# Attention's output product: two fp32 halves on column places against one whole product of split terms on the full array, in every second stretch

## The chip, the core and the metric

The kernel runs on one core of a Trainium2 chip. The metric is the device time of one execution in microseconds (us), median of several runs. The engines named below are TensorE (PE, with its weight loads shown apart as PEld), VectorE (DVE), ScalarE (ACT), GpSimd (POOL) and SyncE (SP), which issues most DMAs. The profiled execution is one run of its own, with its own time.

## The reference: what is computed

```python
x = A_x                                              # 1 x 2048 x 448
g = sigmoid((x * gate_w).sum(-1, keepdims=True))
# a: attention, 16 query heads of 28, one key head and one value head
q = (x @ wq) as 16 heads;  k = x @ wk;  v = x @ wv
p = softmax(q k^T * 28 ** -0.5);  o = p v
a = concat(o) @ wo                                   # 448 -> 448
# b: token shift and MLP mixer
h  = gelu(layernorm(B_x) @ w1), shifted by +1, -1, +2, -2 tokens in four parts
x1 = B_x + shifted(h) @ w2
b  = x1 + gelu(layernorm(x1) @ w3) @ w4              # 448 -> 1792 -> 448
out = g * a + (1 - g) * b
```

All arrays are fp32. Products of fp32 data are made in two ways in this kernel. A plain fp32 matmul appears in the trace as two instructions, each of which streams its columns at half the pace (256 columns in 0.22 us, where 512 columns of a split term take 0.23). A product of split terms uses the type fp32r: each operand is cut into a high part (its value rounded to fp32r) and a low part (what is left), and three matmuls add up high x high, high x low and low x high, each at full pace.

## The kernel before, in words

There are three parts, one behind the other in time: the projections and the token mixing, the MLP, and, from 394 us on, attention. Within `manual_schedule` each engine executes its instructions in the order in which the program issues them, so the order of calls in the last loop is the order on each engine. SP's DMA queue is in order as well.

**Attention** has 16 units (`NU`). Unit `u` is one block of 512 tokens and one group of 4 heads (for the last four units `place` swaps the meaning of tile and group). Each unit has 8 stretches (`NV`), and stretch `k = 8 u + v` takes two tiles of 128 keys. A stretch of the loop at L1050 issues, in order:

- `exps` (L1011): `scores` of the first key tile into the banks `even` (three tiles of PSUM: `even[0]`, `even[1]` with two banks, `even[2]`), one bank for each head. The four heads lie on four row places of the array, with 28 to 30 rows each, 512 columns, in three rounds of split terms. Then ACT makes exponentials from `even[0]` and from `even[1]` (L1009), DVE copies `even[2]` to `pd` (L1015). Then the same for the second key tile in the banks `odd`: DVE copies `odd[1]` (L1018) and ACT makes exponentials of the three banks of `odd[0]`.
- `late_exps` (L1021): ACT's exponential of what DVE has copied.
- one job in a PSUM bank that has just been freed: in the first stretches a rest of the MLP (`w4_job`, `w4_half`), later the output product `wo`.
- `values` (L1034) of the stretch before: sums of p times v, in fp32, on four column places (head j gives rows 32 j to 32 j + 31), for two halves of 256 tokens and two key tiles. One key tile in one half is one call of `value`: four matmuls, which the trace shows as eight. DVE adds each half to `o` (L1032) as soon as it is there.
- on some stretches the work on the unit before: row sums to a DRAM tile and back as reciprocals (`sums_begin` at v = 0, `recip` at v = 1), and at v = 3 `norm`, in which DVE writes the normalised `on` (128 rows of head and value dimension x 512 tokens).

**The output product** of a unit is 512 tokens x 448 columns, with the 128 rows of its 4 heads as the contraction: four tiles `t` of 128 tokens. `wo_part` (L877) makes a part of it in fp32 with `on` as the stationary operand, on four column places of 32 tokens each. `wo_half` makes 224 of the 448 columns, one half in each stretch from k = 12 on: those of unit u - 1 for v = 4 to 7, and of unit u - 2 for v = 0 to 3. In the last unit, at v = 4, 5 and 6, whole tiles of unit 14 are made (`wo_job` with 448 columns). `wo_end` has DVE read the bank, scale it by the gate and add it to `ot` (`by_one`, L874); with the last group, SP stores `ot`.

**PSUM.** After the scores, `free` lists `even[0], even[2], even[1][:, 0], odd[1]`. The job takes the first of it, and `values` takes the first and the last of what is left. So with a job the product goes to `even[0]`, and the two halves of `values` go to `even[2]` and `odd[1]`; without one they go to `even[0]` and `odd[1]`.

**Other queues.** POOL splits the queries of unit u + 2 (`q_begin` at v = 6), which frees the buffer for the DMA of the next queries (`q_fetch`, on SP). There are three sets of probability tiles (`SETS`), taken in turn, one for each stretch. The tail behind the loop makes the last stretch, one last whole tile of unit 14 and the output product of unit 15.

Of the kernel before, what the change touches and what calls it, by code (L numbers as in the profile page):

```python
# [10 lines left out]
F32R = mybir.dt.float32r  # L11
AF = mybir.ActivationFunctionType
ALU = mybir.AluOpType
# [3 lines left out]
P = 128  # L17
S = 2048
D = 448
# [17 lines left out]
def f32(ap):  # L37
    return ap.bitcast(F32)
# [3 lines left out]
def gated_mix_kernel(  # L42
# [12 lines left out]
    nc = tc.nc  # L55
# [120 lines left out]
    def place(u, t):  # L176
        b, g = divmod(u, NG)
        return (4 * b + t, g) if b < NB - 1 else (4 * b + g, t)
# [25 lines left out]
    NU = NB * NG  # L204
# [56 lines left out]
    with tc.tile_pool(name="s1b", bufs=1) as s1b, \  # L261
# [35 lines left out]
        hh, hl, acts = {}, {}, {}  # L297
# [382 lines left out]
    with tc.tile_pool(name="s2", bufs=1, reuse_waits="tile") as s2, \  # L680
            tc.tile_pool(name="ps2", bufs=1, space=PSUM, reuse_waits="tile") as ps2:
        def weigh_x1(n0, n1):
            for n in range(n0, n1):
                nc.gpsimd.tensor_scalar(x1[:, n, :], x1[:, n, :], gi[:, n:n + 1], None, op0=ALU.mult)
# [43 lines left out]
        for b in range(NB):  # L728
            acc = [ps2.tile([P, 512], F32, tag="acc", bufs=4, name=f"acc_{b}_{t}") for t in range(4)]
            gs = {}  # L730
            for f in range(NF):
# [35 lines left out]
                u = M_AT.get(b * NF + f)  # L767
# [33 lines left out]
    with tc.tile_pool(name="s3", bufs=1, reuse_waits="tile") as s3, \  # L801
            tc.tile_pool(name="ps3", bufs=1, space=PSUM, reuse_waits="tile") as ps3:
        wof = s3.tile([P, 4, D], F32, name="wof")
# [7 lines left out]
        banks = []  # L811

        def take():
            return banks.pop(0)
# [8 lines left out]
        def q_fetch(u):  # L823
            if u >= NU:
                return
            raw = s3.tile([P, 512], F32, tag="qr", bufs=1, name=f"qr_{u}")
            if u < NU - NG:
                q_load(u, raw, 2 if u in TWO_PARTS else 1)
            else:
                q_load_last(u, raw)  # L830

        def q_begin(u):
            q_split(u, s3.tile([P, 512], F32R, tag="qh", bufs=3, name=f"qh_{u}"),
                    s3.tile([P, 512], F32R, tag="ql", bufs=3, name=f"ql_{u}"), nc.gpsimd)

        q_fetch(1)

        on_of = {}

        good = s3.tile([P, 16], F32, name="good")  # L840
        nc.gpsimd.memset(good, 1.0)
# [4 lines left out]
        def sums_begin(u, o):  # L846
            rt = s3.tile([P, 16], F32, tag="rt", bufs=2, name=f"rt_{u}")
            nc.sync.dma_start(rt, o[0:128:32, :].rearrange("j (a b) -> j a b", b=16))
            return u, o, rt
# [12 lines left out]
        def norm(u, o, rb):  # L862
            on_of[u] = s3.tile([P, 512], F32, tag="on", bufs=2, name=f"on_{u}")
            nc.vector.tensor_mul(on_of[u], o, rb)
# [12 lines left out]
        def wo_part(u, t, cols, ps, start, stop):  # L877
            for j in range(4):
                tok = slice(t * P + 32 * j, t * P + 32 * j + 32)
                nc.tensor.matmul(ps[32 * j:32 * j + 32, cols], on_of[u][:, tok], wof[:, place(u, t)[1], cols],  # L880
                                 start=start, stop=stop, tile_position=(0, 32 * j))

        def wo_end(u, t, ps, evict=by_one, queue=nc.sync, cols=slice(0, D)):
            n, g = place(u, t)
            before = x1[:, n, cols] if g == 0 else ot_of[n][:, cols]
            evict(n, ps, before, cols)
            store = out[0, n * P:(n + 1) * P, :], ot_of[n]
            if g == NG - 1 and cols.stop == D and queue:
                queue.dma_start(*store)
            return store  # L890

        def wo_job(u, t, cols=slice(0, D), evict=by_one, queue=nc.sync, ps=None):
            n, g = place(u, t)
            own = ps is None
            if own:
                ps = take()
            wo_part(u, t, cols, ps, True, True)
            if g == 0 and cols.start == 0:
                ot_of[n] = s3.tile([P, D], F32, tag="ot", bufs=5, name=f"ot_{n}")
            store = wo_end(u, t, ps, evict, queue, cols)  # L900
            if own:
                banks.append(ps)
            return store

        def wo_half(u, i, ps):
            t, h = divmod(i, 2)
            wo_job(u, t, slice(224 * h, 224 * h + 224), ps=ps)

        def w4_job(t, ps):
            n = NT - 4 + t  # L910
            tok = slice(t * P, (t + 1) * P)
            gh, gl = last_g
            ps = ps[:, 0:D]
            nc.tensor.matmul(ps, gh[:, tok], w4h[-1][:, 1, :], start=True, stop=False)
            nc.tensor.matmul(ps, gh[:, tok], w4l[-1][:, 1, :], start=False, stop=False)
            nc.tensor.matmul(ps, gl[:, tok], w4h[-1][:, 1, :], start=False, stop=True)
            nc.vector.tensor_add(x1[:, n, :], x1[:, n, :], ps)

        def w4_half(k, i, ps):
            t, h = divmod(i, 2)  # L920
            n = NT - 4 + t
            cols = slice(224 * h, 224 * h + 224)
            for j in range(4):
                tok = slice(t * P + 32 * j, t * P + 32 * j + 32)
                nc.tensor.matmul(ps[32 * j:32 * j + 32, cols], gf_late[k][:, tok], w4f[:, k, cols],
                                 start=True, stop=True, tile_position=(0, 32 * j))
            nc.vector.tensor_add(x1[:, n, cols], x1[:, n, cols], ps[:, cols])
# [44 lines left out]
        p_of, pd_of, o_of, sums, norms = {}, {}, {}, [], []  # L972
        NV = 8
# [37 lines left out]
        def exps(u, v):  # L1011
            pe, po, pd = probabilities(u, v)
            scores(u, 2 * v)
            exp(pe[:, 0, :], even[0])
            nc.vector.tensor_copy(pd[:, 0, :], even[2])  # L1015
            behind[0] = exp(pe[:, 1:3, :], even[1])
            scores(u, 2 * v + 1)
            nc.vector.tensor_copy(pd[:, 1, :], odd[1])  # L1018
            exp(po, odd[0])

        def late_exps(u, v):  # L1021
            pd = pd_of.pop((u, v))
            ins = nc.scalar.activation(pd, pd, AF.Exp, scale=SCALE)  # L1023
            tc.add_manual_dep(ins.ins, behind[0].ins.name, SYNC, reason="one wait of ACT for its own writes per stretch")

        def value(u, kt, i, pv, start, stop):
            for j in range(4):
                nc.tensor.matmul(pv[32 * j:32 * j + 32, HALVES[i]], vext[:, kt, :], p_of[u, kt][j][i],  # L1028
                                 start=start, stop=stop, tile_position=(0, 32 * j))

        def add_value(u, q, pv):
            nc.vector.tensor_add(o_of[u][:, q], o_of[u][:, q], pv[:, q])  # L1032

        def values(u, v, pvs):  # L1034
            if v == 0:
                o_of[u] = s3.tile([P, 512], F32, tag="o", bufs=2, name=f"o_{u}")
            for i, pv in enumerate(pvs):
                q = HALVES[i]
                for kt in (2 * v, 2 * v + 1):
                    value(u, kt, i, pv, kt % 2 == 0, kt % 2 == 1)  # L1040
                if v == 0:
                    nc.vector.tensor_copy(o_of[u][:, q], pv[:, q])
                else:
                    add_value(u, q, pv)
# [5 lines left out]
        for k in range(NU * NV - 1):  # L1050
            u, v = divmod(k, NV)
            if k == 3:
                q_begin(1)
                q_fetch(2)
            if v == 6 and u + 2 < NU:
                q_begin(u + 2)
                q_fetch(u + 3)
            if k == NV + 7:
                weigh_x1(8, NT)
            exps(u, v)  # L1060
            late_exps(u, v)
            free = [even[0], even[2], even[1][:, 0, :], odd[1]]
            if k == 0:
                for t in range(3):
                    w4_job(t, (even[0], even[2], odd[1])[t])
            if k in (2, 3):
                w4_half(1, k + 4, free.pop(0))
            if 4 <= k < 12:
                w4_half(0, k - 4, free.pop(0))
            if v >= 4 and u == NU - 1:  # L1070
                wo_job(NU - 2, v - 4, ps=free.pop(0))
            elif v >= 4 and u:
                wo_half(u - 1, v - 4, free.pop(0))
            if v < 4 and u > 1:
                wo_half(u - 2, v + 4, free.pop(0))
            if k:
                values(*divmod(k - 1, NV), (free[0], free[-1]))
            if u and v == 0:
                sums.append(sums_begin(u - 1, o_of[u - 1]))
            if u and v == 1:  # L1080
                norms.append(recip(*sums.pop()))
            if u and v == 3:
                norm(*norms.pop())
        assert not sums and not norms

        u, v = NU - 1, NV - 1
        o = o_of[u]
# [38 lines left out]
        pvs = [even[0], even[2]]  # L1126
# [19 lines left out]
        for j in range(4):  # L1146
            nc.tensor.matmul(pvs[1][32 * j:32 * j + 32, q1], ident[:, 32 * j:32 * j + 32], o[:, q1],
                             start=False, stop=False, tile_position=(0, 32 * j))
# [8 lines left out]
        n = NT - 1  # L1157
# [78 lines left out]
```

## Time and profile before

| | |
|---|---|
| median of 3 runs | 904.1 us (903.98 to 904.59) |
| profiled execution | 903.88 us, span 902.1 us |
| granted TensorE clock | 1.00 over the whole span |
| PE busy | 897.5 us, 99% of the span |
| ACT busy | 619.6 us, 69% |
| DVE busy | 544.4 us, 60% |
| POOL busy | 105.2 us, 12% |
| attention, from 442 to 877 us (435 us): PE, ACT, DVE, POOL busy | 435.00, 425.34, 300.82, 22.82 us |

The span is the time from the first to the last instruction; what lies around it in the execution is 1.8 us. Busy PE time comes from pipelined matmuls that overlap one another in the record, so it counts short stops as busy too. The starts of the instructions say more: from one weight load or matmul to the next. In the profile's lists, "idle before <- releaser" names what ended the time in which an engine waited, and a group of several instructions of one kind close in time is one row with its count.

### The profile page before, as it was taken

Reading aid. Unit: us, or ns where it says so; the run is one execution under the profiler, and the core shown is the slowest. Engines: PE = TensorE matmul, PEld = TensorE weight load, DVE = VectorE, ACT = ScalarE, POOL = GpSimd, SP = SyncE. Lnnn points to the kernel's source line nnn. Section 1 sums busy time; section 2 is a strip of 40 time slices with the busy share of each in tenths; the row PEclk is TensorE's granted clock in tenths of the full one; section 3 lists DMA queues with packets and bytes.
Section 4 is the critical chain, followed back from the end, with each engine's and each line's share of the span. In section 5 each row is a group of like instructions: output and inputs, shape, how many; then the busy total and the mean of one; then the engine's idle time right before and its main releaser. Section 6 shows DMA issues by size and latency. Waiting matters only on the chain.

```text
span 902.1 us, 23587 instructions
## 1 busy us (share of the span) xinstructions
PE 897.5 (99%) x10091; PEld 645.5 (72%) x10091; DVE 544.4 (60%) x1080; ACT 619.6 (69%) x747; POOL 105.2 (12%) x138
## 2 busy tenths in 40 slices
PE   9999999999999999999999999999999999999998
PEld 7899888888888888875555566665666656666554
DVE  5655374531435746456666676667666667766775
ACT  5443254332231131269999999999999999999996
POOL 3134100221000500015100000000000000000000
PEclk9999999999999999999999999999999999999999
DMA  9876852210222132120000001010011000010000
GB/s 318 303 168 154 235 177 89 61 50 18 51 62 51 38 95 62 31 65 14 27 27 3 26 15 56 25 26 27 2 47 47 26 3 26 15 54 15 25 25 24
DMA packets 52140, 58.20 MB, mean 65 GB/s; under 512 B 9488, under 2 KB 37056, under 8 KB 52032
## 3 DMA queue, kind: packets, MB, share of 16 engines
q1 hardware_dynamic: 48864, 51.07, 20.1%
q10 hardware_dynamic: 3168, 5.59, 1.7%
q8 instruction: 80, 1.31, 0.6%
q14 instruction: 28, 0.23, 0.1%
HBM read 39.80 MB, written 15.59 MB: 61 GB/s over the span
## 4 chain that ended last, share of the span: by engine, by line
PE 99%; ACT 0%; DVE 0%; issue 0%; DVEq 0%
PE even L980 13%; PE even L1028 12%; PE odd L1028 12%; PE odd L980 10%; PE even L880 7%; PE acc L725 5%; PE acc L724 5%; PE acc L726 5%; PE g L132 4%; PE g L131 4%; PE g L133 4%; PE hs L494 1%; PE hs L495 1%; PE g L134 1%; PE g L135 1%; PE hs L497 1%
## 5 line engine op out<-in xcount | busy, mean ns | idle before, releaser
L1009 ACT ACTIVATE pe<-even 128x512 f32<-128x512 f32 (+1 forms) x257 | 193.8, 806 | 12.8 <-PE even L980 2.2
L1009 ACT ACTIVATE po<-odd 128x1536 f32<-128x1536 f32 x129 | 187.0, 1450 | 0.0
L713 ACT ACTIVATE gh<-g 128x512 fp32r<-128x512 f32 x54 | 32.2, 597 | 181.1 <-PE g L135 181.1
L1023 ACT ACTIVATE pd<-pd 128x1024 f32<-128x1024 f32 x127 | 136.2, 1072 | 0.0
L1028 PE MATMUL even<-pd,vext 128*32 128x256 f32 x520 | 133.2, 379 | 0.0
L1028 PE MATMUL odd<-pd,vext 128*32 128x256 f32 x504 | 129.4, 379 | 0.0
L1015 DVE COPY pd<-even 128x512 f32<-128x512 f32 x127 | 87.7, 690 | 53.1 <-PE even L980 53.1
L716 DVE TENSOR_TENSOR gl<-gf,gh 128x512 fp32r<-128x512 f32 x54 | 37.2, 688 | 118.1 <-ACT gf L714 118.0
L1018 DVE COPY pd<-odd 128x512 f32<-128x512 f32 x127 | 87.8, 692 | 0.0
L1028 PE MATMUL even<-pe,vext 128*32 128x256 f32 x780 | 79.2, 379 | 0.0
L1028 PE MATMUL even<-po,vext 128*32 128x256 f32 x780 | 79.1, 379 | 0.0
L725 PE MATMUL acc<-w4l,gh 128*128 128x448 f32 x216 | 79.0, 366 | 0.0
L724 PE MATMUL acc<-w4h,gh 128*128 128x448 f32 x216 | 78.9, 365 | 0.0
L726 PE MATMUL acc<-w4h,gl 128*128 128x448 f32 x216 | 78.7, 365 | 0.0
L1028 PE MATMUL odd<-pe,vext 128*32 128x256 f32 x756 | 76.7, 379 | 0.0
L1028 PE MATMUL odd<-po,vext 128*32 128x256 f32 x756 | 76.6, 379 | 0.0
L1032 DVE TENSOR_TENSOR o<-o,odd 128x256 f32<-128x256 f32 x110 | 46.3, 421 | 48.6 <-PE odd L1028 48.6
L880 PE MATMUL even<-wof,on 128*32 128x224 f32 (+1 forms) x952 | 70.6, 369 | 0.0
L1032 DVE TENSOR_TENSOR o<-o,even 128x256 f32<-128x256 f32 x111 | 46.8, 422 | 39.1 <-PE even L1028 38.8
L132 PE MATMUL g<-al,w3h 128*128 128x512 f32 x168 | 65.8, 392 | 0.0
L131 PE MATMUL g<-ah,w3h 128*128 128x512 f32 x168 | 65.6, 391 | 0.0
L133 PE MATMUL g<-ah,w3l 128*128 128x512 f32 x168 | 65.5, 390 | 0.0
(240 smaller groups left out, 1833.8 us busy)
## 6 DMA issues: line engine op xcount, KB each, us to landing
qd<-qf ACTq DMA_DIRECT2D x16, 256.0 KB
qm<-qd SPq DMA_DIRECT2D x16, 256.0 KB
rb<-rd SPq DMA_DIRECT2D x15, 256.0 KB
x<-in_x_dram SPq DMA_DIRECT2D x4, 896.0 KB
hd<-ht SPq DMA_DIRECT2D x16, 224.0 KB
hr<-hd SPq DMA_DIRECT2D x8, 448.0 KB
w34raw<-in_w_dram SPq DMA_DIRECT2D x7, 512.0 KB
w34raw<-in_w_dram SPq DMA_DIRECT2D x7, 448.0 KB
```

The costliest lines, as they stand in the source:

```text
L131: nc.tensor.matmul(ps, wh[:, c, :], ah[:, c, :], start=(c == 0), stop=False)
L132: nc.tensor.matmul(ps, wh[:, c, :], al[:, c, :], start=False, stop=False)
L133: nc.tensor.matmul(ps, wl[:, c, :], ah[:, c, :], start=False, stop=False)
L724: nc.tensor.matmul(ps, gh[:, tok], w4h[i][:, k, :], start=(f == 0), stop=False)
L725: nc.tensor.matmul(ps, gh[:, tok], w4l[i][:, k, :], start=False, stop=False)
L726: nc.tensor.matmul(ps, gl[:, tok], w4h[i][:, k, :], start=False, stop=(f == stop))
L880: nc.tensor.matmul(ps[32 * j:32 * j + 32, cols], on_of[u][:, tok], wof[:, place(u, t)[1], cols], start=start, stop=stop, tile_position=(0, ...
L980: nc.tensor.matmul(bs[j], w, a, start=(i == 0), stop=(i == 2), tile_position=(32 * j, 0))
L1009: return nc.scalar.activation(p, ps, AF.Exp, scale=SCALE)
L1023: ins = nc.scalar.activation(pd, pd, AF.Exp, scale=SCALE)
L1028: nc.tensor.matmul(pv[32 * j:32 * j + 32, HALVES[i]], vext[:, kt, :], p_of[u, kt][j][i], start=start, stop=stop, tile_position=(0, 32 * j))
L1032: nc.vector.tensor_add(o_of[u][:, q], o_of[u][:, q], pv[:, q])
```

## The change

Of each two stretches from k = 13 on, the one with odd v has an output job and the one with even v has none. A job is one whole tile, 128 tokens x 448 columns, as three matmuls in fp32r on the full array (`wo_split`): the high and the low part of `on` are the stationary operands (128 x 128), the high and the low part of `wo` the moving ones. For that, POOL splits `wo` once (`split_wo`, at k = 5 to 8, one group each) and each `on` behind its `norm` (`split_on`, at v = 3). DVE reads the 448 columns of the bank in one instruction. In a stretch with a job, `values` leaves the first half of its second key tile to the next stretch, which adds it in front of its own two (`left_over`): two rounds fewer in one stretch, two more in the next. In the last unit, jobs stand at v = 1 and 3 and then at v = 4, 5 and 6, each whole; from v = 3 of that unit on nothing is left over. The tail is as before.

```diff
+        on_of, on2_of = {}, {}
+        wof2 = [s3.tile([P, 4, D], F32R, name=f"wof{n}") for n in "hl"]
+
+        def split_wo(g):
+            nc.gpsimd.tensor_copy(wof2[0][:, g, :], wof[:, g, :])
+            nc.gpsimd.tensor_tensor(wof2[1][:, g, :], wof[:, g, :], f32(wof2[0])[:, g, :], ALU.subtract)
+
+        def split_on(u):
+            onh, onl = on2_of[u] = [s3.tile([P, 512], F32R, tag=f"on{n}", bufs=2, name=f"on{n}_{u}") for n in "hl"]
+            nc.gpsimd.tensor_copy(onh, on_of[u])
+            nc.gpsimd.tensor_tensor(onl, on_of[u], f32(onh), ALU.subtract)
...
+        def wo_split(u, t, cols, ps, start, stop):
+            (onh, onl), (wh, wl) = on2_of[u], wof2
+            g = place(u, t)[1]
+            tok = slice(t * P, (t + 1) * P)
+            for n, (a, w) in enumerate(((onh, wh), (onh, wl), (onl, wh))):
+                nc.tensor.matmul(ps[:, cols], a[:, tok], w[:, g, cols], start=start and n == 0, stop=stop and n == 2)
...
-        def wo_job(u, t, cols=slice(0, D), evict=by_one, queue=nc.sync, ps=None):
+        def wo_job(u, t, ps):
             n, g = place(u, t)
...
+            wo_split(u, t, slice(0, D), ps, True, True)
+            if g == 0:
                 ot_of[n] = s3.tile([P, D], F32, tag="ot", bufs=5, name=f"ot_{n}")
...
+            wo_end(u, t, ps)
...
-        def values(u, v, pvs):
+        left_over = []
+
+        def values(u, v, pvs, shift):
...
             for i, pv in enumerate(pvs):
                 q = HALVES[i]
-                for kt in (2 * v, 2 * v + 1):
-                    value(u, kt, i, pv, kt % 2 == 0, kt % 2 == 1)
+                kts = [2 * v, 2 * v + 1]
+                if i == 0:
+                    kts = left_over + kts
+                    left_over[:] = [kts.pop()] if shift else []
+                for kt in kts:
+                    value(u, kt, i, pv, kt == kts[0], kt == kts[-1])
...
+            if 5 <= k < 9:
+                split_wo(k - 5)
+            job, shift = None, False
             if v >= 4 and u == NU - 1:
-                wo_job(NU - 2, v - 4, ps=free.pop(0))
-            elif v >= 4 and u:
-                wo_half(u - 1, v - 4, free.pop(0))
-            if v < 4 and u > 1:
-                wo_half(u - 2, v + 4, free.pop(0))
+                job = u - 1, v - 4
+            elif v % 2 and k >= NV + 5:
+                job = (u - 1, (v - 5) // 2) if v >= 5 else (u - 2, (v + 3) // 2)
+                shift = (u, v) != (NU - 1, 3)
+            if job:
+                wo_job(*job, free.pop(0))
             if k:
-                values(*divmod(k - 1, NV), (free[0], free[-1]))
+                values(*divmod(k - 1, NV), (free[0], free[-1]), shift)
...
             if u and v == 3:
                 norm(*norms.pop())
+                split_on(u - 1)
```

More of the change, by code (lines that the diff above doesn't have):

```diff
@@ L836, in gated_mix_kernel @@
         q_fetch(1)
-        on_of = {}
+        on_of, on2_of = {}, {}
[7 more added lines that the diff above has]
+            nc.gpsimd.tensor_tensor(onl, on_of[u], f32(onh), ALU.subtract)
         good = s3.tile([P, 16], F32, name="good")
@@ L890, in wo_end @@
             return store
-        def wo_job(u, t, cols=slice(0, D), evict=by_one, queue=nc.sync, ps=None):
+        def wo_job(u, t, ps):
             n, g = place(u, t)
[L894 to L898, printed above, removed]
-                ot_of[n] = s3.tile([P, D], F32, tag="ot", bufs=5, name=f"ot_{n}")
[L900 to L907, printed above, removed]
+            wo_split(u, t, slice(0, D), ps, True, True)
+            if g == 0:
+                ot_of[n] = s3.tile([P, D], F32, tag="ot", bufs=5, name=f"ot_{n}")
+            wo_end(u, t, ps)
         def w4_job(t, ps):
@@ L1083, in gated_mix_kernel @@
                 norm(*norms.pop())
-        assert not sums and not norms
+                split_on(u - 1)
+        assert not sums and not norms and not left_over
         u, v = NU - 1, NV - 1
```

## The prediction

> **What bounds the kernel now.** I read the page's head and its chain of waits first, then one stretch of attention in order of time, then the places where the trace already shows the operations that the change brings.
>
> ```profile
> span 902.1 us, 23587 instructions
> PE 897.5 (99%) x10091; PEld 645.5 (72%) x10091; DVE 544.4 (60%) x1080; ACT 619.6 (69%) x747; POOL 105.2 (12%) x138
> PE 99%; ACT 0%; DVE 0%; issue 0%; DVEq 0%
> ```
>
> The chain is PE throughout. But PE's record has overlapping pipelined matmuls, so "busy" hides short stops. They show between starts. One stretch (k = 66), from its first score weight load to that of the next; the columns are start, duration, engine, line, operation:
>
> ```profile
> 650.63 0.19 PEld L980 LDWEIGHTS even<-qh,kH 30*128 30x128 f32 x4 [0.41 <-DVE o L1042]
> ...
> 651.62 1.51 ACT L1009 ACTIVATE pe<-even 128x512 f32<-128x512 f32 x2
> ...
> 651.89 0.41 PE L980 MATMUL odd<-ql,kH 28*128 28x512 f32 x4
> 652.27 0.16 PEld L880 LDWEIGHTS even<-wof,on 128*32 128x32 f32 x8 [0.40 <-ACT pe L1009]
> 652.28 0.59 PE L880 MATMUL even<-wof,on 128*32 128x224 f32 x8
> ...
> 652.68 0.39 PE L1028 MATMUL even<-pe,vext 128*32 128x256 f32 x3
> ...
> 653.00 0.45 DVE L874 SCALAR_TENSOR_TENSOR ot<-even,gg,ot 128x224 f32<-128x224 f32 x1
> 653.02 1.46 ACT L1009 ACTIVATE po<-odd 128x1536 f32<-128x1536 f32 x1
> ...
> 654.19 0.39 PE L1028 MATMUL odd<-po,vext 128*32 128x256 f32 x3
> ...
> 654.35 1.07 ACT L1023 ACTIVATE pd<-pd 128x1024 f32<-128x1024 f32 x1
> ...
> 654.52 0.19 PEld L980 LDWEIGHTS even<-qh,kH 30*128 30x128 f32 x4 [0.41 <-DVE o L1032]
> ```
>
> and, by form, ACT's first exponential of a stretch:
>
> ```profile
> L1009 ACT ACTIVATE pe<-even 128x512 f32<-128x512 f32 x106 | 63.3, 597 | 9.1
> ```
>
> So a stretch has three pieces. **Head:** from the score weights to the first work behind the scores, 652.27 - 650.63 = 1.64 us. It ends when ACT has read `even[0]`: 651.62 + 0.60 = 652.22, and the weight load follows 0.05 later. The last round of scores began at 651.89 and streams for 0.23, so PE had been done at 652.12: the head is set by ACT's release, not by the array. **Work:** the half product, 652.68 - 652.27 = 0.41, then eight rounds of `values`, of which seven take 654.19 - 652.68 = 1.51 (0.216 each). **Turn:** from the last round to the next score weights, 654.52 - 654.19 = 0.33, a round and 0.11 of gap. Sum: 1.64 + 0.41 + 1.51 + 0.33 = 3.89.
>
> The chain, in order of time, gives the mean: its first piece with the half product and the first whole one are 112 stretches apart.
>
> ```profile
> 442.37 0.57 PE even L880 x8
> ...
> 877.54 0.92 PE even L880 x8
> ...
> 881.79 0.94 PE even L880 x8
> ```
>
> (877.54 - 442.37) / 112 = 3.885 us, or 7.77 for two stretches. ACT has room: its starts in the stretch give 1.40 + 1.33, and where it waits for nothing but itself, at k = 2 below, 0.95 from the copied part to the next start; its floor is 3.68.
>
> **The change part by part.** Its products are in the trace already: at k = 0 of attention three rests of the MLP are made as three split terms on the full array, behind the same scores and into the same `even[0]`; k = 1 has no job at all.
>
> ```profile
> 396.01 0.19 PEld L914 LDWEIGHTS even<-w4h,gh_late 128*128 128x128 f32 x1 [0.40 <-ACT pe L1009]
> 396.01 0.47 PE L914 MATMUL even<-w4h,gh_late 128*128 128x448 f32 x1
> ...
> 396.32 0.36 PE L915 MATMUL even<-w4l,gh_late 128*128 128x448 f32 x1
> ...
> 396.52 0.36 PE L916 MATMUL even<-w4h,gl_late 128*128 128x448 f32 x1
> ...
> 397.73 0.37 PE L916 MATMUL odd<-w4h,gl_late 128*128 128x448 f32 x1
> 398.03 0.35 PEld L980 LDWEIGHTS even<-qh,kH 30*128 30x128 f32 x4 [0.30 <-issue]
> ...
> 399.78 0.12 PEld L1028 LDWEIGHTS even<-pe,vext 128*32 128x32 f32 x3 [0.35 <-ACT pe L1009]
> ...
> 400.02 0.39 PE L1028 MATMUL even<-pe,vext 128*32 128x256 f32 x3
> ...
> 401.81 1.07 ACT L1023 ACTIVATE pd<-pd 128x1024 f32<-128x1024 f32 x1
> ...
> 402.76 1.52 ACT L1009 ACTIVATE pe<-even 128x512 f32<-128x512 f32 x2
> ```
>
> *Stretch with a job.* Head 1.64, since the product again waits for `even[0]`. First term 396.32 - 396.01 = 0.31: its 128 columns of weights are loaded only behind ACT's release, and nothing covers them. Second term 0.20. Then the third term and the step from the full array to column places, which I call s and which the trace lacks. Bounds: 0.20 if the step costs nothing (the pace of these terms), 0.36 if the matmul must be out of the array (its duration). The nearest row is full array to row places, 398.03 - 397.73 = 0.30, with 0.10 of gap; the turn from column to row places has a gap of 0.11. I take s = 0.30. Then six rounds of values: the first 400.02 - 399.78 = 0.24 with its uncovered weights, four steps of 0.216, and the turn 0.33. Sum: 1.64 + 0.31 + 0.20 + 0.30 + 0.24 + 0.86 + 0.33 = 3.88.
>
> The Trainium skill, "TensorEngine Tiling (Array Packing)", Key Properties, says that a change of tiling mode drains the array; by that rule the step has a price, as in the 0.30 of 398.03, and the sum stays as it is; without it s would be 0.20, and 55 times 0.10, an estimate of 5.5 us, would go.
>
> *Stretch without.* Head 1.64 again: its first round goes to `even[0]`, which ACT releases, where it went to `even[2]` before. Ten rounds: 0.24, eight steps of 0.216, turn 0.33. Sum 3.94.
>
> The pair takes 3.88 + 3.94 = 7.82, against 7.77: **+0.05**. The halves looked dear at 0.57 in the chain, but 0.15 of that is the head's end, which a stretch without a job pays as well. Really 2 x 0.41 = 0.82 go, and 0.31 + 0.20 + 0.30 come, with two first rounds of 0.24 in place of two of 0.216. There are 55 such pairs: +2.8 us.
>
> *DVE behind the product* sets nearly the same length on another way. The product ends at 1.64 + 0.31 + 0.20 + 0.36 = 2.51 in its stretch; DVE starts 0.13 after an end (652.28 + 0.59 against 653.00), at 2.64. Rows of the last unit, where DVE reads 448 columns now:
>
> ```profile
> 876.34 0.69 DVE L864 TENSOR_TENSOR on<-o,rb 128x512 f32<-128x512 f32 x1
> ...
> 877.51 0.16 PEld L880 LDWEIGHTS even<-wof,on 128*32 128x32 f32 x8 [0.40 <-ACT pe L1009]
> ...
> 878.63 0.68 DVE L874 SCALAR_TENSOR_TENSOR ot<-even,gg,x 128x448 f32<-128x448 f32 x1 [0.34 <-PE even L880]
> ...
> 879.40 0.42 DVE L1032 TENSOR_TENSOR o<-o,even 128x256 f32<-128x256 f32 x1
> ```
>
> The add of the first half follows 0.77 after, at 3.41, ends at 3.83 and releases `even[2]` at 3.88 for the fourth score matmul of the next stretch, about where PE comes by itself. Before, this add was over 0.3 before it was asked for; now even s = 0.20 would leave the stretch near 3.87, and the pair at +0.04.
>
> *Ends of the run of pairs.* k = 12 loses its half and gets nothing: PE needs 1.64 + 0.24 + 1.30 + 0.33 = 3.51, ACT 3.68, so -0.20. At unit 15, v = 3 there is a job and nothing is left over: 3.88 + 2 x 0.216 = 4.31, +0.43. At v = 4 to 6 the same 4.31 stands against 881.79 - 877.54 = 4.25: +0.06 each, +0.18. Together +0.4.
>
> *POOL.* The splits cost, by its rows for queries,
>
> ```profile
> L196 POOL TENSOR_TENSOR ql<-qr,qh 128x512 fp32r<-128x512 f32 x12 | 15.5, 1289 | 1.0
> L195 POOL CAST qh<-qr 128x512 fp32r<-128x512 f32 x12 | 7.3, 612 | 333.0 <-PE odd L980 333.0
> ```
>
> 0.61 + 1.29 = 1.90 us for each `on`. POOL is idle for 333 us in these rows alone, and from v = 3 to the first job at v = 5 there is a whole stretch of 3.89: hidden, at nothing. `split_wo` lies five stretches ahead of its use. POOL's next split of queries and SP's fetch behind it now stand behind `norm`, v = 3, and are wanted a unit later. Without this cover the price shows once: in the last unit the job comes at v = 4. `on` is there at 876.34 + 0.69 = 877.03, its high part at 877.7, the low part at 879.0. The third term, due at 877.51 + 0.31 + 0.20 = 878.02, starts behind 879.0 + 0.05 with 0.11 of uncovered weights, at 879.16: **+1.1 us**, during which the values and all scores behind it on PE wait, and ACT for those.
>
> `left_over` needs a probability tile one stretch longer. Three sets are there, the writer comes behind scores that PE makes after the left round: nothing. As many DMAs are issued as before.
>
> **Sum:** 2.8 + 0.4 + 1.1 = +4.3 on the profiled execution's 903.88 us (its span 902.1 and 1.8 around it): 908.2. The median of the runs lies 0.2 above that execution: **908.4 us**.
>
> **Rivals.** (1) *The step is dearer:* s = 0.36, the array must be empty, or DVE starts later than 0.13 (in the last unit 878.63 lies 0.17 behind the product's end). Each pair +0.11, 6.1 us, total 911.7. For it: nothing in the rows runs from the full array to column places. Against: the step to row places cost 0.30. Chance 0.17. (2) *No step, and DVE holds nothing up:* s = 0.20 and the pair at -0.05, -2.8 + 1.5 = -1.3, 902.8. Both must hold; 398.03 speaks against the first and the sum above against the second. Chance 0.12. (3) *Faster:* the weights of the first term are loaded ahead, while PE waits for ACT, which takes its 0.31 to 0.20, and the step costs nothing. DVE then releases at 3.77, the job's stretch is 3.76, the pair -0.07: -3.9 + 1.5 = -2.4, 901.7; if DVE's add slips too, 3.67 and -0.16, -7.3, 896.8. It decides once more than 0.03 a pair is won, that is with a job stretch under 3.80. Against it: at 396.01 the load itself waits for ACT and the first term starts with it. Chance 0.11. The Trainium skill, "TensorE: Matmul & The Clock Gate", Architectural detail, says that PE's queue can take weight loads ahead of running matmuls, which would be this case; the row at 396.01 shows none.
>
> **How the numbers follow.** Forecast 0.60, rivals 0.17, 0.12, 0.11. The range from 902.6 to 912.3 takes in the forecast's own bounds (+0.03 to +0.09 a pair: 907.2 to 910.6), the dear step and part of no step, and leaves the rest out. About 0.2%, 1.8 us, is what can be told from no change here: 902.3 to 905.9 is the same. The forecast and the first rival lie above it, 0.77, of which 0.02 goes inside for a smaller stall in the last unit with short pairs: 0.75 slower. The second rival lies inside, with that 0.14 the same. The third is below: 0.11 faster.
>
> **What would show it.** Weight load of a job 0.05 behind ACT's release in both kinds of stretch (the head at 1.64). First to second term 0.31. From the third term's start to the first weights of values: s. Ten rounds in the stretch without a job, pair of stretches 7.82 long against 7.77. The add of the first half ending at 3.83, next to the scores that need its bank. One wait of PE for POOL, at unit 15, v = 4, of about 1.1 us. I am wrong if pairs come under 7.74, or if POOL holds up PE in every unit.

## The result, and the profile after

The changed kernel takes 910.74 us (median of 4 runs, 910.39 to 911.16), against 904.26 us of the kernel before in the same comparison: ratio 1.0072, 95% interval 1.0054 to 1.0089. It is slower by 6.5 us. Forecast were 908.4 us, in a range from 902.6 to 912.3, and slower with a chance of 0.75.

The head of the page after:

```profile
span 908.6 us, 22048 instructions
PE 901.9 (99%) x9348; PEld 640.8 (71%) x9348; DVE 535.6 (59%) x1024; ACT 619.0 (68%) x747; POOL 139.5 (15%) x176
PE 98%; issue 0%; DVE 0%; POOL 0%; ACT 0%; DVEq 0%; ACTq 0%; POOLq 0%
```

PE has 743 matmul records fewer and yet is on the chain as before. The span grew by 6.5 us, all of it in attention. One pair of stretches (k = 65 and 66) in order of time; the columns are start, duration, engine, line, operation:

```profile
649.69 1.51 ACT L1016 ACTIVATE pe<-even 128x512 f32<-128x512 f32 x2 [0.15 <-PE even L987]
...
650.34 0.19 PEld L898 LDWEIGHTS even<-wofh,onh 128*128 128x128 f32 x1 [0.42 <-ACT pe L1016]
...
650.45 0.19 PEld L898 LDWEIGHTS even<-wofl,onh 128*128 128x128 f32 x1
650.65 0.37 PE L898 MATMUL even<-wofl,onh 128*128 128x448 f32 x1
...
650.86 0.36 PE L898 MATMUL even<-wofh,onl 128*128 128x448 f32 x1
...
651.15 0.12 PEld L1035 LDWEIGHTS even<-pe,vext 128*32 128x32 f32 x3 [0.30 <-DVE pd L1025]
...
651.33 0.68 DVE L884 SCALAR_TENSOR_TENSOR ot<-even,gg,ot 128x448 f32<-128x448 f32 x1 [0.20 <-PE even L898]
...
651.93 0.41 DVE L1055 COPY o<-even 128x256 f32<-128x256 f32 x1
...
652.58 0.19 PEld L987 LDWEIGHTS even<-qh,kH 30*128 30x128 f32 x4 [0.41 <-DVE o L1055]
...
653.59 1.51 ACT L1016 ACTIVATE pe<-even 128x512 f32<-128x512 f32 x2
...
654.24 0.12 PEld L1035 LDWEIGHTS even<-po,vext 128*32 128x32 f32 x3 [0.42 <-ACT pe L1016]
...
656.53 0.19 PEld L987 LDWEIGHTS even<-qh,kH 30*128 30x128 f32 x4 [0.41 <-DVE o L1039]
...
658.19 0.19 PEld L898 LDWEIGHTS even<-wofh,onh 128*128 128x128 f32 x1 [0.42 <-ACT pe L1016]
```

The stretch with a job takes 652.58 - 650.34 = 2.24 us behind its head. In it the first term lasts 0.31, the second 0.21, and from the third term to the first weights of `values` pass 0.29. The stretch without takes 656.53 - 654.24 = 2.29 behind its head. Both heads are 1.66 (654.24 - 652.58, 658.19 - 656.53). The pair is 7.85.

Over all pairs, and through the last unit, by the chain in order of time (start, length, piece):

```profile
453.86 0.86 PE even L898 x3
...
878.26 0.84 PE even L898 x3
...
888.16 0.86 PE even L898 x3
...
896.80 2.83 PE even L1035 x48
```

(878.26 - 453.86) / 54 = 7.86 a pair. In the kernel before, the same 108 stretches lie between these two pieces of the chain:

```profile
454.06 0.57 PE even L880 x8
...
873.66 0.55 PE even L880 x8
```

They take 873.66 - 454.06 = 419.60 us, or 7.77 for two. The 6.5 us lie as follows: -0.2 up to k = 15, **+4.8** in the 54 pairs, **+1.8** in the two stretches k = 123 and 124 (9.90 against 881.79 - 873.66 = 8.13), +0.1 in the next two, nothing behind.

In the second of those two stretches, unit 15 at v = 4, POOL's splits are late; the rows of POOL and of PE's weight loads there:

```profile
882.20 0.61 POOL L847 CAST onh<-on 128x512 fp32r<-128x512 f32 x1 [29.87 <-DVE on L874]
882.89 1.28 POOL L848 TENSOR_TENSOR onl<-on,onh 128x512 fp32r<-128x512 f32 x1
```

```profile
882.87 0.19 PEld L898 LDWEIGHTS even<-wofh,onh 128*128 128x128 f32 x1 [0.73 <-POOL onh L847]
...
884.22 0.19 PEld L898 LDWEIGHTS even<-wofh,onl 128*128 128x128 f32 x1 [1.06 <-POOL onl L848]
```

The third term's weights wait 1.06 us for the low part. And in every unit the first job, at v = 5, waits for POOL and for ACT. In unit 8, in order of time:

```profile
664.33 1.30 POOL L196 TENSOR_TENSOR ql<-qr,qh 128x512 fp32r<-128x512 f32 x1
...
665.39 1.51 ACT L1016 ACTIVATE pe<-even 128x512 f32<-128x512 f32 x2 [0.15 <-PE even L987]
...
666.11 0.19 PEld L898 LDWEIGHTS even<-wofh,onh 128*128 128x128 f32 x1 [0.48 <-POOL ql L196]
```

POOL's last work ends at 665.63, and its split of `on` lies ahead of that in its order, yet the load comes 666.11 - (665.39 + 0.60) = 0.12 behind ACT's release, where it comes 0.05 behind it elsewhere (650.34 - 649.69 - 0.60). The packed trace shows what lies between. At each first job, and at no other job of the 54 pairs, it has one more instruction on PE ahead of the weight load, an EVENT_SEMAPHORE of L898, which the profile's lists leave out. It holds the wait for ACT (in unit 8 it stands at 666.03 for 0.05), and the weight load behind it the wait for POOL; at the other jobs the weight load itself holds the wait for ACT. In all 14 first jobs the load comes 0.11 behind ACT's release, in the other jobs 0.05. So the 0.06 is the wait for a second engine made as an instruction of its own behind ACT's release, not POOL's lateness.

### The profile page after: what moved, and what is told of

It reads as the page before. It is cut to its first block, busy times and chain, and to the rows that moved or that the text cites. A ratio compares the mean times of both kernels' runs of the same rounds, so it can differ in the third digit from the quotient of the medians.

```text
span 908.6 us, 22048 instructions
## 1 busy us (share of the span) xinstructions
PE 901.9 (99%) x9348; PEld 640.8 (71%) x9348; DVE 535.6 (59%) x1024; ACT 619.0 (68%) x747; POOL 139.5 (15%) x176
## 3 DMA queue, kind: packets, MB, share of 16 engines
q10 hardware_dynamic: 3168, 5.59, 1.7%
## 4 chain that ended last, share of the span: by engine, by line
PE 98%; issue 0%; DVE 0%; POOL 0%; ACT 0%; DVEq 0%; ACTq 0%; POOLq 0%
PE even L1035 14%; PE even L987 12%; PE odd L1035 12%; PE odd L987 10%; PE even L898 5%; PE acc L725 5%; PE acc L724 5%; PE acc L726 5%; PE g L132 4%; PE g L131 4%; PE g L133 4%; PE hs L494 1%; PE hs L495 1%; PE g L134 1%; PE g L135 1%; PE hs L497 1%
## 5 line engine op out<-in xcount | busy, mean ns | idle before, releaser
L1035 PE MATMUL even<-pd,vext 128*32 128x256 f32 x520 | 136.0, 385 | 0.0
L847 POOL CAST onh<-on 128x512 fp32r<-128x512 f32 x15 | 9.1, 610 | 406.1 <-DVE on L874 378.2
```

## The experiments

The theory: PE is bound by order and not by columns. A split product on the full array saves 0.15 of columns and pays 0.11 for a weight load that nothing covers and 0.09 for the change of the array's form; the pairing costs another bit. The rivals: the pairing and the left-over round are what costs; or the wait for ACT keeps the weights uncovered, not the array's form; or it is POOL.

**The product in fp32 on column places, all else as in the change.**

```diff
-            wo_split(u, t, slice(0, D), ps, True, True)
+            wo_part(u, t, slice(0, D), ps, True, True)
```

> The changed kernel, but each whole output product is made in fp32 on the four column places from the unsplit operands, as in the kernel before; pairing, left-over round and POOL's splits stay (the splits are not read). Theory (the product's form costs: 0.11 of uncovered weights and 0.09 of step against 0.15 fewer columns): the stretch with a job has 0.78 of product and six rounds, 2.19 behind its head in place of 2.24, the wait for POOL goes at v = 5 (0.06 each) and in the last unit (1.2), pair 7.79, total 905.5 us. Rival (the pairing and the left-over round cost, not the form): only the stall goes, total about 909.4 us.

Measured: 904.77 us against 904.71, ratio 1.000 (0.999 to 1.0009). A stretch with a job, in order of time:

```profile
648.46 0.16 PEld L890 LDWEIGHTS even<-wof,on 128*32 128x32 f32 x8 [0.42 <-ACT pe L1016]
648.46 0.96 PE L890 MATMUL even<-wof,on 128*32 128x448 f32 x8
...
649.24 0.39 PE L1035 MATMUL even<-pe,vext 128*32 128x256 f32 x3
...
650.65 0.19 PEld L987 LDWEIGHTS even<-qh,kH 30*128 30x128 f32 x4 [0.41 <-DVE o L1055]
```

It takes 650.65 - 648.46 = 2.19 behind the head, as expected, with 0.78 for the whole product in fp32. A pair takes 7.78 by the trace, against 7.77 in the kernel before. So pairing and left-over round by themselves are worth nothing either way, to within 0.1%: the bit that the theory gave to the pairing is not there. The whole loss goes with the split product, its form and type, and what it needs of POOL.

**One change of form more: the product between the two halves of `values`.** The first half goes to `even[0]`, the product to `even[2]`, which DVE has freed by then.

```diff
-            if job:
-                wo_job(*job, free.pop(0))
             if k:
-                values(*divmod(k - 1, NV), (free[0], free[-1]), shift)
+                values(*divmod(k - 1, NV), (free[0], free[-1]), shift,
+                       (lambda: wo_job(*job, free[1])) if job else None)
...
+                if i == 0 and between:
+                    between()
```

> The changed kernel, with the product between the two halves of values in its stretch: the first half goes to even[0], the product to even[2], which is free by then, so it waits for nobody and its weights could be loaded early. Theory (a change of the array's form stops the array and keeps the weights of the next form out): one change more in each pair, 0.24 + 0.33 + 0.31 + 0.20 + 0.29 + 0.24 + 0.76 = 2.37 behind the head against 2.24, pair +0.13, total 917.5 us. Rival (only the wait for ACT keeps the first weights uncovered): first term 0.20 and no gap ahead of it, 2.16 behind the head, total 906 us.

Measured: 915.96 us, ratio 1.0122 (1.0105 to 1.0139). A stretch with a job, in order of time:

```profile
652.52 0.69 DVE L1022 COPY pd<-even 128x512 f32<-128x512 f32 x1 [0.51 <-PE even L987]
...
653.09 0.12 PEld L1035 LDWEIGHTS even<-pe,vext 128*32 128x32 f32 x3 [0.41 <-ACT pe L1016]
...
653.33 0.39 PE L1035 MATMUL even<-pe,vext 128*32 128x256 f32 x3
...
653.66 0.19 PEld L898 LDWEIGHTS even<-wofh,onh 128*128 128x128 f32 x1 [0.41 <-DVE pd L1022]
...
653.97 0.37 PE L898 MATMUL even<-wofl,onh 128*128 128x448 f32 x1
...
655.47 0.19 PEld L987 LDWEIGHTS even<-qh,kH 30*128 30x128 f32 x4 [0.41 <-DVE ot L884]
```

The bank was free at 652.52 + 0.69 = 653.21, and the weights come at 653.66 all the same: 0.33 behind the last round of values, a round of 0.22 and a gap of 0.11, as at the turn to the scores. Nothing but the array was in the way. And though PE waited for nobody, the first term still took 0.31. So in fp32r the uncovered weight load belongs to the change of form, not to ACT's release. 655.47 - 653.09 = 2.38 against 2.37 expected; the rival falls. Over all pairs the trace has 7.97, which is 0.11 more than in the change and not 0.13, and the total stays 1.5 us under the 917.5 expected. Here too an EVENT_SEMAPHORE stands at each first job, but the load waits for no release of ACT, and the stretches with a first job are no longer than the others (4.02).

**Nothing left over: eight rounds of `values` in each stretch.**

```diff
-                shift = (u, v) != (NU - 1, 3)
```

> The changed kernel without the left-over round: eight rounds of values in each stretch, with a job or without. Theory (ACT needs 3.68 for a stretch, so a stretch of 3.52 on PE gives ACT's lateness to the next, as at k = 12 and 13 of the changed kernel, where 3.52 is followed by 0.23 more): pair 3.52 + 4.33 + 0.23 = 8.08, total about 922.5 us. Rival (ACT has room and the left-over round does nothing but cost a round's weights): pair 7.83, total about 909.5 us.

Measured: 918.73 us, against 922.5 expected; ratio 1.0152 (1.0131 to 1.0172). The chain in order of time, one pair:

```profile
653.97 0.87 PE even L898 x3
...
658.31 1.09 PE even L1035 x16
...
660.37 1.07 ACT pd L1030
661.44 0.49 ACT pe L1016
...
661.98 0.87 PE even L898 x3
```

Here ACT appears on the chain: the stretch without a job is too short for it. The pair takes 661.98 - 653.97 = 8.01. I expected 8.08: the 0.23 of lateness that I took from k = 13 has the 0.06 of a first job in it, and heads of 1.82 in place of 1.66 leave 0.17. The rival falls. So with the split product the left-over round is what keeps the pairing from costing; it earns its place.

**The last unit's first tile in fp32.**

```diff
-            wo_split(u, t, slice(0, D), ps, True, True)
+            if (u, t) == (NU - 2, 0):
+                wo_part(u, t, slice(0, D), ps, True, True)
+            else:
+                wo_split(u, t, slice(0, D), ps, True, True)
```

> The changed kernel, with the first tile of the last unit's product (unit 15, v = 4) in fp32 on column places from the unsplit operands. Theory: that stretch takes 4.26 in place of 5.59, total 1.3 us less than the changed kernel, 909.4 us. Rival (the stall only moves to the next tile, v = 5): the same total as the changed kernel, 910.7 us.

Measured: 909.17 us against 904.8, ratio 1.0047 (1.003 to 1.0063), where the change has 1.0072: the intervals overlap, so the times alone do not settle it. By the trace the stretch takes 4.43 in place of 5.59, and the two behind it 8.70 in place of 8.63: 1.1 us are won and not 1.3, and the stall does not move on. (The profiled span, 907.3, is 1.3 below the 908.6 of the change, but 0.3 of that lies ahead of k = 13, where the two kernels are alike.) The stretch did not come down to 4.26: `on` itself came later here, since DVE waited 0.45 for the DMA of the reciprocals (it started at 881.68, 1.01 behind the stretch's first weights, where in the change that was 0.48), and the load came 0.17 behind ACT's release in place of 0.05. The stall is a price of its own, paid once.

**Split terms on column places.** This was tried in bf16, not in fp32r. High and low part then carry some 16 bits together, less than in fp32r, so this and the following kernels make the output product less exactly than the change does. First the type alone, on the full array:

```diff
-        wof2 = [s3.tile([P, 4, D], F32R, name=f"wof{n}") for n in "hl"]
+        wof2 = [s3.tile([P, 4, D], BF16, name=f"wof{n}") for n in "hl"]
...
-            onh, onl = on2_of[u] = [s3.tile([P, 512], F32R, tag=f"on{n}", bufs=2, name=f"on{n}_{u}") for n in "hl"]
+            onh, onl = on2_of[u] = [s3.tile([P, 512], BF16, tag=f"on{n}", bufs=2, name=f"on{n}_{u}") for n in "hl"]
```

> The changed kernel with its split terms in bf16 on the full array (less exact than fp32r, as above), which alone changes the type. Theory: the columns stream at the same pace; the first term's uncovered weight load shrinks with the type or not. If it stays at 0.11, the total is that of the changed kernel, 910.7 us; if it falls to 0.03, each pair is 0.08 shorter, 906.3 us. In both cases the step from the full array to column places stays at 0.29.

Measured: 901.15 us, ratio 0.9959 (0.9945 to 0.9973): more is won than the 906.3 that I gave the weight load at best. A stretch with a job, in order of time:

```profile
644.89 1.51 ACT L1017 ACTIVATE pe<-even 128x512 f32<-128x512 f32 x2
...
645.16 0.40 PE L988 MATMUL odd<-ql,kH 28*128 28x512 f32 x4
645.49 0.15 PEld L899 LDWEIGHTS <-onh 128*128 128x128 bf16 x2 [0.37 <-issue]
645.54 0.35 PE L899 MATMUL even<-wofh,onh 128*128 128x448 bf16 x1
...
645.73 0.35 PE L899 MATMUL even<-wofl,onh 128*128 128x448 bf16 x1
...
645.92 0.35 PE L899 MATMUL even<-wofh,onl 128*128 128x448 bf16 x1
646.20 0.12 PEld L1036 LDWEIGHTS even<-pe,vext 128*32 128x32 f32 x3 [0.37 <-issue]
```

The weight load no longer waits for ACT: its row names no output bank and no ACT, and it comes 645.49 - 645.16 = 0.33 behind the last round of scores, a round of 0.23 and a gap of 0.10. Only the matmul waits, to 645.54, which is 0.05 behind ACT's release (644.89 + 0.60), and the second term follows after 0.19. So the 0.31 of the first term fell to 0.19, each of the others lost 0.01 to 0.02, and the load's way into the array is hidden in the wait. The 0.06 of the first jobs is gone as well: these stretches take 3.74, as the others with a job. A pair takes 7.70 by the trace, against 7.86. The step from the full array to column places is still there, 646.20 - 645.92 = 0.28.

Then the form as well, in pairs as in the change:

```diff
-            tok = slice(t * P, (t + 1) * P)
             for n, (a, w) in enumerate(((onh, wh), (onh, wl), (onl, wh))):
-                nc.tensor.matmul(ps[:, cols], a[:, tok], w[:, g, cols], start=start and n == 0, stop=stop and n == 2)
+                for j in range(4):
+                    tok = slice(t * P + 32 * j, t * P + 32 * j + 32)
+                    nc.tensor.matmul(ps[32 * j:32 * j + 32, cols], a[:, tok], w[:, g, cols],
+                                     start=start and n == 0, stop=stop and n == 2, tile_position=(0, 32 * j))
```

> The changed kernel, with the split terms in bf16 and on the four column places (bf16 carries fewer bits than fp32r: high and low part together some 16, so the product is less exact). Theory: without a change of the array's form and with weights of 32 columns, three terms of 448 columns take 0.215 + 2 x 0.19, the stretch with a job 2.00 behind its head, near ACT's floor of 3.68, pair 7.60 to 7.63, total 897.5 to 899 us. Rival (the full array's form costs nothing, what is lost is lost to pairing and to POOL): pair as in the changed kernel, 7.85, total about 910 us.

Measured: 897.31 us, ratio 0.9917 (0.99 to 0.9933), just under the theory's lower end; the rival's 910 is out. A stretch with a job, in order of time:

```profile
644.53 0.37 PE L900 MATMUL even<-wofh,onh 128*32 128x448 bf16 x4
...
644.91 0.38 PE L900 MATMUL even<-wofh,onl 128*32 128x448 bf16 x4
...
645.10 0.40 PE L1038 MATMUL even<-pe,vext 128*32 128x256 f32 x3
...
646.50 0.19 PEld L990 LDWEIGHTS even<-qh,kH 30*128 30x128 f32 x4 [0.41 <-DVE o L1058]
```

From the third term to `values` pass 645.10 - 644.91 = 0.19, a term and nothing more, where the full array in the same type had 0.28. So the step belongs to the change of form, and costs 0.09. By the trace the stretch with a job takes 3.63, which is 0.11 less than with bf16 on the full array; the one without takes 4.01, 0.06 more, since ACT with its floor of 3.68 is late into it. A pair is left with 7.64, against 7.70.

And by halves in every stretch, without pairs and without the left-over round (a job is now a unit, its first half and the half where it ends; `wo_job`, not shown, takes these):

```diff
-            if v >= 4 and u == NU - 1:
-                job = u - 1, v - 4
-            elif v % 2 and k >= NV + 5:
-                job = (u - 1, (v - 5) // 2) if v >= 5 else (u - 2, (v + 3) // 2)
-                shift = (u, v) != (NU - 1, 3)
+            if u == NU - 1:
+                job = ((u - 2, 3, 4), (u - 2, 4, 6), (u - 2, 6, 7), (u - 2, 7, 8),
+                       (u - 1, 0, 2), (u - 1, 2, 4), (u - 1, 4, 6))[v]
+            elif v >= 5 and u:
+                job = u - 1, v - 5, v - 4
+            elif u > 1:
+                job = u - 2, v + 3, v + 4
```

> Split terms in bf16 on the four column places, and half products in every stretch as in the kernel before, one stretch later because of the splits (from v = 5 on); nothing is left over, and in the last unit three wholes and one more make up for the stretch. Theory: a half takes 0.025 + 3 x 0.095 = 0.31 in place of 0.41, stretch 3.79, over ACT's floor of 3.68, 108 of them: -10 us, with 1.7 us back for POOL's waits: total 895.5 to 896.5 us. Rival (short terms are bound by their weight loads, 0.11 a term): 0.36 a half, total 899 to 900 us.

Measured: 892.58 us, ratio 0.9863 (0.9846 to 0.9879), 3 us under the theory's lower end. One stretch in order of time:

```profile
640.74 0.19 PEld L992 LDWEIGHTS even<-qh,kH 30*128 30x128 f32 x4 [0.41 <-DVE o L1044]
...
642.35 0.16 PEld L900 LDWEIGHTS <-onh 128*32 128x32 bf16 x8 [0.37 <-issue]
642.39 0.28 PE L900 MATMUL even<-wofh,onh 128*32 128x224 bf16 x4
...
642.68 0.40 PE L1040 MATMUL even<-pe,vext 128*32 128x256 f32 x3
...
644.52 0.19 PEld L992 LDWEIGHTS even<-qh,kH 30*128 30x128 f32 x4 [0.41 <-DVE o L1060]
```

A half takes 642.68 - 642.39 = 0.29 in place of 0.41, and the stretch 3.78, as expected; at under 0.10 a term the short terms are not bound by their weights. From k = 15 to 123 the trace has 10.9 us less than before. What I had added to that for POOL's waits, 1.7 us, was too much: here the weights do not wait for ACT, a wait for POOL lies ahead of ACT's release, and the first jobs' stretches take 3.78 like the others.

**Both together:** the halves above, with unit 14's first tile in fp32, as in the experiment on the last unit.

> Bf16 split terms on column places by halves in every stretch (as before, less exact than fp32r), and the first tile of unit 14, which the last unit wants one stretch after its normalisation, in fp32 from the unsplit operand. Theory: the stall for POOL there goes (that stretch took 5.22 where the next whole one took 4.06), 4.25 + 0.06 are left: 0.9 us less than without this, 891.7 us. Rival (the wait goes to the next tile): 892.6 us, as without.

Measured: 891.77 us (891.61 to 892.24), ratio 0.9857 (0.984 to 0.9873). The difference to the run before is 0.8 us, and the intervals of the two overlap; but the trace shows the stall gone, with 4.27 for that stretch in place of 5.22, and 8.10 in place of 8.12 for the two behind it, so it did not move on. This beats both kernels, by 13 and 19 us, at the price of bf16 terms in the output product. Whether an application may pay it is for its owner; with fp32r none of these runs was faster than the kernel before.

## Why the prediction was right, point by point

- **The order of the stretch, not the columns, sets the time:** right. Behind the heads, the two stretches of the pair measure 2.24 and 2.29; the working had 2.24 and 2.30. The first term measures 0.31, as at k = 0. The total, 910.7 us, lies at the upper end of the forecast's own bounds (910.6) and nearer to the first rival's 911.7 than to 908.4, so the time alone would not tell the two apart; the rows below do.
- **The step s from the full array to column places:** taken as 0.30 from the row of full array to row places, measured 0.29. That a step to column places costs as much as one to row places could not be read from any row beforehand; it came out so. The first rival's 0.36 and the second's 0.20 are out, and so is the rival's later DVE: it starts 651.33 - (650.86 + 0.36) = 0.11 behind the product. By the drain that the Trainium skill's "TensorEngine Tiling (Array Packing)", Key Properties, names, a gap is due at each change; the rows show one of 0.08 to 0.11 each time, and with one change more a stretch was longer by 0.14, the uncovered weights of `values` included.
- **The heads:** a term of the sum that was mis-sized. I kept 1.64 for both; they measure 1.66 in the pair shown, and in the mean over the 54 pairs 1.652 with a job (first jobs left out) and 1.657 without, where the kernel before has 1.642. The difference arises ahead of ACT's first exponential, which starts 653.59 - 652.58 = 1.01 behind the first score weights, against 651.62 - 650.63 = 0.99 before; behind it both kernels need 0.65. In 108 heads this is some 1.6 us of the 2.1 that the pairs cost more than forecast (4.8 against 54 times 0.05). Heads of both lengths occur in the kernel before too (446.25 - 444.60 = 1.65 in the first jobs), and with the product between the halves they fell back to about 1.645, so nothing shows that the split product makes them longer; what decides it stays open.
- **POOL at nothing except in the last unit:** wrong by a small size. The data were there in time, but the first job of each unit pays 0.06 for a second wait, some 0.8 us over 13 units. One of the prediction's signs of being wrong, that POOL holds up PE in every unit, is met to that extent. Heads and first jobs together make 2.4, somewhat over the 2.1; the sums go by two decimals. In the last unit 1.6 us were forecast for both stretches (0.43 + 0.06 + 1.1), 1.8 measured.
- **DVE as a second bound of nearly the same length:** this step failed. It had the add of the first half follow 0.77 behind DVE's read of the product, from a row of the last unit. There the add came 0.07 behind the modelled end of PE's four rounds for the first half (878.95 + 0.38), so it was waiting for PE. In the change, with two rounds for that half, it follows after 0.60 (651.33, 651.93), 0.08 before DVE's read is over, and ends at 652.34, 0.24 ahead of the next scores, though their row names DVE as the last to release. DVE never held the pair up, and the sum did not rest on it.
- **The third rival, weights loaded ahead:** not in fp32r, whose first load waited for ACT at each job, and came late even where nobody had to be waited for. In bf16 it went ahead of ACT's release, though not ahead of the scores. What the Trainium skill's "TensorE: Matmul & The Clock Gate", Architectural detail, says of weight loads taken ahead of matmuls in flight agrees with the rows within one form (the second term's load at 650.45 comes 0.20 ahead of its own term at 650.65, while the first still runs); it does not show in the first load of a new form, in fp32r (650.34) or in bf16 (645.49). The prediction's 0.03 a pair for this rival is where the total would be even; to come out of the 0.2% takes 0.06 (55 times 0.06 is 3.3, less the 1.5 of the ends).
- **k = 12:** -0.20 forecast. It took 3.52, 0.38 less than before, and gave 0.17 of ACT's lateness to k = 13; up to k = 15 the change is ahead by 0.20.

The forecast's mechanism held; 4.3 us became 6.5, by some 2.1 in the pairs, with their heads and first jobs, and 0.2 in the last unit.

## What to carry to other kernels

Price an operation between neighbours of another array form by its surroundings: read from weight load to weight load what the switch in and out costs, before counting columns. Here 0.15 us of columns were bought with 0.20 of uncovered weights and gaps; where the form stayed the same, the shorter product was won (0.29 a half in place of 0.41, at fewer bits). Where the chain shows a step as dear, see first whether part of it is a wait that stays when the step goes: 0.15 of the half product's 0.57 was the head's end, and the stretch without a job paid it as well.

## What the runs showed that I had not expected

The bf16 weight load did not wait for the output's bank and went into PE's wait for ACT; the fp32r one waited. Together with a pace faster by 0.01 to 0.02 a term, and with the first jobs' 0.06 gone, this made 9.6 us between two kernels that differ in one type (910.74 and 901.15, ratios 1.0072 and 0.9959). And where the weight load had POOL to wait for besides ACT, the wait for ACT became an instruction of its own, and the load came 0.06 us later, though POOL was done before ACT.
